# Agent attention with expert rows on one core: the order of the instructions as a literal list instead of a list scheduler with a table of ranks

## The chip, the cores and the metric

The kernel runs on one core of a Trainium2 chip. The metric is the device time of one execution in microseconds (us); lower is better. The core has five instruction queues that matter here: TensorE (PE in the profile, with its weight loads as PEld), VectorE (DVE), ScalarE (ACT), GpSimd (POOL) and SyncE (SP), which issues almost all transfers. Each queue runs its own instructions strictly in the order in which the program holds them and waits at each for the semaphores it needs.

## The reference, cut to what matters

```python
# q, k, v: 4 x 12608 x 128 fp32; agents: 4 x 49 x 128
a2k    = softmax(scale * agents @ k.T)        # 49 x 12608 per batch, over all keys
agentv = a2k @ v                              # 49 x 128
q2a    = softmax(scale * q @ agents.T)        # 12608 x 49, over the 49 agents
x      = q2a @ agentv                         # 12608 x 128
# then, per batch: the 128 rows of x with the largest x . w_gate get
scores = x @ w_gate
top    = argpartition(-scores, 128)[:128]
out    = x                                    # all other rows as they are
out[top] = x[top] + sigmoid(scores[top]) * (relu(x[top] @ w1) @ w2)   # w1 128x1024, w2 1024x128
```

## The kernel before

**Tiles.** A batch's 12608 tokens are 99 columns of 128 tokens, cut into seven chunks (six of 15 columns, chunk 6 of 9). The inputs lie transposed or padded in HBM, so a chunk of k, q or v is one load of 960 KB (967.5 KB for v; 576 and 580.5 KB for chunk 6) into one of six buffers (`inp`, N_IN = 6), a chunk of the result is one store of 960 KB. There are 84 such loads and 28 such stores.

**Work per chunk.** For a k chunk: two halves of scores, each four matmuls of 32 agents by 480 tokens into one of three PSUM banks (tile `S`); DVE turns each half into `sk` and takes its maximum (`mx`). After all seven chunks of a batch the common maximum `mb` is made on PE and DVE (`mT`, `mB`); POOL then subtracts it from each `sk`, ACT takes the exponent. For a v chunk: 15 steps that sum `av` on PE, two instructions each. After the seventh, a chain of small steps (`pw`, `pp`) gives the weights `ws`. For a q chunk: two halves of `S` again, DVE turns them into `sq` and takes a row maximum (`qm`); POOL subtracts, ACT takes the exponent and a rounded copy `f`, POOL subtracts the copy for the low part of `f`; PE transposes `f` (`fT`, 15 instructions), ACT or DVE copies it out as `ft`. From `ft` and `ws` come the gate scores (`pg`, 15 instructions of 3 columns) and the output (`po`, 30 instructions), which ACT, DVE and POOL scale into `og`, and SP stores. Per batch a selection of the 128 best rows follows (`all`, `gt`, `pc`), and at the end the expert rows (`qT`, `sc`, `eT`, `xT`, `xe`, `ph`, `py`), whose results POOL scatters into the output (`out<-ey`) after the batch's stores have landed.

**What sets the order.** All these steps are first recorded as operations with their dependencies (class `Recorder`), 1466 in all. `place` then runs a list scheduler over them: it keeps a price of each operation, a price of a change from one kind of PE work to another (`switch`), a model of TensorE's clock (`Clock`) and of the transfers, and at each moment starts on each free engine the ready operation with the smallest rank. The rank is a number per step and engine from the table `RANKS`, less STICK if the operation is of the kind that the engine did last. The operations are then issued in that order, all from line 1435, so that every row of the profile has that line:

```python
    order = place(rec, urgency, SLACK, STICK)
    ...
    with tc.manual_schedule():
        for op in order:
            for call, args, kwargs in op.calls:
                call(*args, **kwargs)
```

The prices decide the order while the program is built; nothing of them is executed on the chip.

## Time and profile before

| | us |
|---|---|
| three runs of the kernel before | 289.36, 289.97, 291.24 (median 289.97) |
| the profiled execution, its own time | 289.3 |
| its span, from first to last instruction | 287.4 |
| TensorE busy in the span | 266.9 (93%) |
| DVE, ACT, POOL busy | 224.3, 171.6, 183.4 |
| moved over the span | 106.68 MB, 371 GB/s on average |

All later rows are of that one profiled execution; 1.9 us of its time lie outside its span. A row of the profile says how long a group of instructions kept an engine busy; what it had waited for stands in brackets behind it, after an arrow. A row that waits for nothing in brackets began when the instruction before it on that engine let it.

### The profile page before, as it was taken

How to read it: one execution, taken by the hardware profiler on the slowest of the kernel's cores; microseconds unless marked ns; L12 is line 12 of the kernel's file. 1: busy time of each engine (PE TensorE's matmuls, PEld its weight loads, DVE VectorE, ACT ScalarE, POOL GpSimd, SP SyncE). 2: the span in 40 equal slices, each digit the busy share in tenths (PEclk: the TensorE clock that was granted, in tenths of full speed). 3: DMA queues.
4: the chain of work that ended last, by engine and by line, in shares of the span. 5: the costliest groups of instructions: out<-in, count | busy, mean ns of one | idle time of the engine just before them, and what ended most of it. 6: DMA issues, size and time to landing. Idle time of an engine off the chain costs nothing.

```text
span 287.4 us, 8559 instructions
## 1 busy us (share of the span) xinstructions
PE 266.9 (93%) x3524; PEld 176.3 (61%) x3524; DVE 224.3 (78%) x517; ACT 171.6 (60%) x313; POOL 183.4 (64%) x152
## 2 busy tenths in 40 slices
PE   1985798999999999999999999999999999999992
PEld 0221235594557645536455974656798789898992
DVE  1897897977999888997788979558925869998730
ACT  1004156553168965518496988979979854975500
POOL 8014799894189999119998329998422234784723
PEclk9999799999999999999999999889999999999997
DMA  7999999999999999999999999999813585999981
GB/s 281 424 408 419 422 426 415 422 417 422 418 421 391 380 423 410 408 421 412 418 423 419 421 422 414 413 420 373 320 52 148 222 349 220 414 413 408 419 372 48
DMA packets 18203, 106.68 MB, mean 371 GB/s; under 512 B 2032, under 2 KB 3440, under 8 KB 18160
## 3 DMA queue, kind: packets, MB, share of 16 engines
q1 hardware_dynamic: 17760, 105.42, 90.1%
q8 instruction: 30, 0.49, 0.7%
q0 software_dynamic: 256, 0.52, 0.5%
q10 hardware_dynamic: 144, 0.13, 0.1%
q14 instruction: 13, 0.11, 0.1%
HBM read 79.85 MB, written 26.21 MB: 369 GB/s over the span
## 4 chain that ended last, share of the span: by engine, by line
PE 65%; POOL 12%; DMA 9%; ACT 7%; DVE 3%; issue 3%; POOLq 0%; ACTq 0%
PE S L1435 24%; PE av L1435 13%; PE po L1435 13%; PE fT L1435 6%; POOL sk L1435 5%; DMA xT<-kT 4%; DMA out<-og 3%; POOL f L1435 3%; PE pg L1435 2%; PE all L1435 2%; ACT gt L1435 2%; PE ph L1435 2%; POOL sq L1435 2%; DMA ag_sb<-agT 2%; ACT ft L1435 2%
## 5 line engine op out<-in xcount | busy, mean ns | idle before, releaser
L1435 PE MATMUL S<-xT,ag_sb 128*32 128x480 f32 (+1 forms) x896 | 102.4, 572 | 10.8 <-DMA ag_sb<-agT 6.0
L1435 POOL TENSOR_TENSOR sq<-sq,qm 128x735 f32<-128x735 f32 (+1 forms) x42 | 56.9, 1368 | 34.9 <-DVE qm L1435 27.8
L1435 PEld LDWEIGHTS <-ft 128*128 128x128 f16 x1188 | 59.1, 98 | 15.1 <-issue 13.3
L1435 POOL TENSOR_TENSOR f<-sq,f 128x735 f16<-128x735 f32 (+1 forms) x28 | 42.7, 1527 | 23.5 <-ACT f L1435 21.2
L1435 PEld LDWEIGHTS S<-xT,ag_sb 128*32 128x32 f32 x896 | 23.5, 111 | 54.1 <-issue 24.6
L1435 PE MATMUL po<-ws,ft 128*128 128x128 f16 x792 | 53.5, 220 | 0.5 <-ACT og L1435 0.4
L1435 POOL TENSOR_TENSOR sk<-sk,mb 128x735 f32<-128x735 f32 (+1 forms) x28 | 47.2, 1703 | 8.8 <-DVE mb L1435 8.8
L1435 PE MATMUL av<-v,sk 128*64 128x129 f32 x792 | 49.9, 275 | 0.4 <-DMA v<-va 0.4
L1435 PEld LDWEIGHTS av<-v,sk 128*64 128x64 f32 x792 | 44.5, 136 | 8.5 <-DMA v<-va 3.6
L1435 ACT COPY ft<-fT 128x896 f16<-128x896 f16 (+2 forms) x49 | 43.7, 896 | 8.8 <-PE fT L1435 8.6
L1435 DVE STREAM_TRANSPOSE sq<-S 128x480 f32<-128x480 f32 (+1 forms) x56 | 35.5, 639 | 11.6 <-POOL f L1435 8.4
L1435 DVE STREAM_TRANSPOSE sk<-S 128x480 f32<-128x480 f32 (+1 forms) x56 | 35.1, 635 | 6.3 <-PE S L1435 3.5
L1435 DVE TENSOR_REDUCE qm<-sq 128x15 f32<-128x735 f32 (+1 forms) x42 | 36.1, 865 | 1.2 <-ACT sq L1435 0.7
L1435 ACT ACTIVATE sq<-sq,lift 128x735 f32<-128x735 f32 (+1 forms) x28 | 25.0, 891 | 19.5 <-POOL sq L1435 19.3
L1435 DVE TENSOR_REDUCE mx<-S 128x1 f32<-128x480 f32 (+1 forms) x56 | 33.0, 607 | 3.1 <-PE S L1435 2.9
L1435 POOL TENSOR_TENSOR og<-og,r 128x512 f32<-128x512 f32 (+1 forms) x26 | 24.3, 944 | 14.1 <-ACT og L1435 13.9
L1435 PEld LDWEIGHTS <-f 128*128 128x128 f16 x396 | 22.9, 98 | 12.2 <-issue 7.6
L1435 ACT ACTIVATE sk<-sk 128x735 f32<-128x735 f32 (+1 forms) x28 | 22.4, 799 | 12.4 <-POOL sk L1435 12.2
L1435 PE MATMUL fT<-idh,f 128*128 128x128 f16 x396 | 28.8, 220 | 0.8 <-POOL f L1435 0.8
L1435 ACT CAST f<-sq 128x735 f16<-128x735 f32 (+1 forms) x28 | 22.2, 793 | 11.1 <-POOL sq L1435 10.5
L1435 ACT ACTIVATE og<-po,iv 128x512 f32<-128x512 f32 (+1 forms) x28 | 18.0, 663 | 12.6 <-PE po L1435 11.5
L1435 DVE SCALAR_TENSOR_TENSOR gt<-all,top,minus 128x512 bf16<-128x512 f32 x32 | 23.6, 739 | 0.9 <-PE all L1435 0.5
(131 smaller groups left out, 251.2 us busy)
## 6 DMA issues: line engine op xcount, KB each, us to landing
v<-va SPq DMA_DIRECT2D x24, 967.5 KB, 8.8
xT<-kT SPq DMA_DIRECT2D x24, 960.0 KB, 9.1
xT<-qT SPq DMA_DIRECT2D x24, 960.0 KB, 9.0
out<-og SPq DMA_DIRECT2D x24, 960.0 KB, 6.4
v<-va SPq DMA_DIRECT2D x4, 580.5 KB, 6.9
xT<-kT SPq DMA_DIRECT2D x4, 576.0 KB, 8.8
xT<-qT SPq DMA_DIRECT2D x4, 576.0 KB, 9.1
out<-og SPq DMA_DIRECT2D x4, 576.0 KB, 5.6
```

The lines of the kernel that those rows point to most:

```text
L1435: call(*args, **kwargs)
```

## The change

The list scheduler, its clock model and the table of ranks are removed. In their place stands a literal list of 1466 numbers, the recorded operations in the order in which they are issued. `place` now only looks the operations up and asserts that each comes after what it depends on. The recorded operations and their shapes are the same, and so are the prices in `price` (which no longer set anything at build time). One dependency is written out: the copy into `f` now names the two memsets that clear the `f` buffers once.

```diff
-SLACK = 0.0
-STICK = 10922.517314977244
-HALF = ("po", "fT", "pg")
[...]
-def place(rec, urgency, slack=0.0, stick=0.0):
...
-RANKS = {
-    ('setup', 0): {"ACT": -7704.603, "POOL": -40854.573, "DVE": -34695.979},
...
+ORDER = (
+    409, 6, 10, 12, 3, 0, 9, 131, 132, 133, 134, 135, 16, 122, 136, 17, 58, 59, 18, 19, 61, 137, 60, 20, 22,
...
+def place(rec):
+
+    order, done = [rec.ops[i] for i in ORDER], set()
+    for op in order:
+        assert op.deps <= done, op.label
+        done.add(op.seq)
+    assert len(done) == len(rec.ops)
+    return order
...
+    zeros = set()
     for i in range(N_F):
         f = qp.tile([P, TMAX, P], F16, tag="f", name=f"f0_{i}", bufs=N_F)
-        nc.gpsimd.memset(f, 0.0)
+        zeros.add(nc.gpsimd.memset(f, 0.0).seq)
...
-        copy(f[:, :n, :A], d["q", c][:, :n, :A])
+        copy(f[:, :n, :A], d["q", c][:, :n, :A]).deps.update(zeros)
...
-    order = place(rec, urgency, SLACK, STICK)
+    order = place(rec)
```

In the rows of order below, a name is a tile, then its chunk, then its half (for `S`), then a running number that sets the batches apart; `xT` is a load of k or q, `v` one of v, and x4 or x15 stands for that many matmuls in a row.

On PE, where the first v chunks of batch 1 are summed (`av_277`), before:

```order
L1435 MATMUL S_0_0_374<-xT_0_373,ag_sb 32x480 x4
L1435 MATMUL S_0_1_375<-xT_0_373,ag_sb 32x480 x4
L1435 MATMUL av_277<-v_0_276,sk_0_242 64x129 x15
L1435 MATMUL all_0_232<-idf,top_226 128x128 x4
L1435 MATMUL S_1_0_378<-xT_1_377,ag_sb 32x480 x4
L1435 MATMUL av_277<-v_1_278,sk_1_246 64x129 x15
L1435 MATMUL av_277<-v_2_279,sk_2_250 64x129 x15
L1435 MATMUL S_3_0_322<-xT_3_321,ag_sb 32x480 x4
L1435 MATMUL S_3_1_323<-xT_3_321,ag_sb 32x480 x4
L1435 MATMUL S_1_1_379<-xT_1_377,ag_sb 32x480 x4
```

The same place on PE, now:

```order
L1123 MATMUL S_2_1_383<-xT_2_381,ag_sb 32x480 x4
L1123 MATMUL S_3_0_322<-xT_3_321,ag_sb 32x480 x4
L1123 MATMUL av_277<-v_0_276,sk_0_242 64x129 x15
L1123 MATMUL av_277<-v_1_278,sk_1_246 64x129 x15
L1123 MATMUL av_277<-v_2_279,sk_2_250 64x129 x15
L1123 MATMUL av_277<-v_3_280,sk_3_254 64x129 x15
L1123 MATMUL pc_234<-c_0_228,idf 128x8
L1123 MATMUL pc_234<-c_0_229,idf 128x8
L1123 MATMUL S_3_1_323<-xT_3_321,ag_sb 32x480 x4
L1123 MATMUL S_4_0_331<-xT_4_330,ag_sb 32x480 x4
L1123 MATMUL S_0_0_505<-xT_0_504,ag_sb 32x480 x4
```

Four v chunks that stood in three runs, with a fourth chunk further on, now stand in one run of 60 steps; the last row is the first half of k chunk 0 of batch 3, whose load `xT_0_504` stood later before.

On SP, the loads that belong to this stretch, before:

```order
L1435 DMA v_0_276<-va 128x1935
L1435 DMA xT_2_312<-qT 128x1920
L1435 DMA xT_0_373<-kT 128x1920
L1435 DMA v_2_279<-va 128x1935
L1435 DMA v_1_278<-va 128x1935
L1435 DMA xT_3_321<-qT 128x1920
L1435 DMA v_5_282<-va 128x1935
L1435 DMA v_3_280<-va 128x1935
```

On SP, the same stretch now:

```order
L1123 DMA v_3_280<-va 128x1935
L1123 DMA xT_3_321<-qT 128x1920
L1123 DMA v_0_276<-va 128x1935
L1123 DMA v_1_278<-va 128x1935
L1123 DMA v_2_279<-va 128x1935
L1123 DMA xT_4_330<-qT 128x1920
L1123 DMA xT_0_504<-kT 128x1920
```

The four v loads of the run now stand within five loads of each other, one other load between them.

On SP, the last loads and the weights of the experts (`w_held`), before:

```order
L1435 DMA xT_4_591<-qT 128x1920
L1435 DMA w_held<-w 128x896
L1435 DMA xT_6_609<-qT 128x1152
L1435 DMA w_held<-w 128x7x128
L1435 DMA xT_3_582<-qT 128x1920
L1435 DMA v_0_537<-va 128x1935
L1435 DMA out<-og_5_660 128x1920
L1435 DMA v_4_542<-va 128x1935
```

On SP, the end of the loads now:

```order
L1123 DMA xT_5_600<-qT 128x1920
L1123 DMA v_5_543<-va 128x1935
L1123 DMA v_6_544<-va 128x1161
L1123 DMA out<-og_0_669 128x1920
L1123 DMA w_held<-w 128x896
L1123 DMA w_held<-w 128x7x128
L1123 DMA out<-og_4_655 128x1920
L1123 DMA out<-og_6_665 128x1152
```

The two loads of `w_held`, 448 KB each, moved behind the last load of the inputs.

Of the kernel before, what the change touches and what calls it, by code (L numbers as in the profile page):

```python
# [28 lines left out]
A = 49  # L29
# [19 lines left out]
SLACK = 0.0  # L49
STICK = 10922.517314977244  # L50
# [202 lines left out]
HALF = ("po", "fT", "pg")  # L253
WINDOW, STAY, RISE = 3413.333, 0.45, 0.76
WORK = {"S": 1.0, "av": 0.89, "po": 0.93, "pg": 0.25, "fT": 0.8, "all": 0.83, "ph": 0.9}
RATE, GATHER, SCATTER = 408.0, 6500.0, 2400.0


def switch(a, b):

    if a in HALF and b in HALF:
        return 10.0
    return 160.0 if a == "av" else 100.0 if a == "S" or b in ("S", "av") else 50.0


def lag(a, b):

    if a.engine == b.engine:
        return 0.0 if a.engine == "PE" else a.tail
    return a.tail + 70.0  # L270


class Clock:


    def __init__(self):
        self.window, self.did, self.full = 0, 0.0, False

    def cost(self, op, t):
        while t >= (self.window + 1) * WINDOW:  # L280
            self.full = self.did >= (STAY if self.full else RISE) * WINDOW
            self.window, self.did = self.window + 1, 0.0
        few = op.kind == "pg"
        c = op.cost * (1.0 if self.full or few else 2.0)
        over = max(0.0, t + c - (self.window + 1) * WINDOW)
        self.did += (c - over) * WORK.get(op.kind, 0.5)
        if over:
            self.full = self.did >= (STAY if self.full else RISE) * WINDOW
            self.window, self.did = self.window + 1, over * WORK.get(op.kind, 0.5)
        return c  # L290


def place(rec, urgency, slack=0.0, stick=0.0):

    ops = rec.ops
    users, takes = {}, [[] for _ in ops]
    for op in ops:
        for name in sorted(op.uses):
            if name not in users:
                takes[op.seq].append(rec.rings[name][0])  # L300
            users.setdefault(name, []).append(op)
    rank = [(urgency(op.tag, op.engine), op.seq) for op in ops]
    room = {ring: bufs for ring, bufs in rec.rings.values()}
    left = {name: len(u) for name, u in users.items()}
    after = [[] for _ in ops]
    missing = [len(op.deps) for op in ops]
    for op in ops:
        for d in op.deps:
            after[d].append(op)
    ready = [0.0] * len(ops)  # L310
    queue = {e: [op for op in ops if op.engine == e and not op.deps] for e in ENGINES.values()}
    free = dict.fromkeys(queue, 0.0)
    last = dict.fromkeys(queue, "")
    times, ends, order = [0.0], [], []
    line, clock = 0.0, Clock()
    while len(order) < len(ops) or ends:
        if not times:
            raise RuntimeError("no instruction can begin")
        now = heapq.heappop(times)
        while ends and ends[0][0] <= now + 1e-6:  # L320
            op = ops[heapq.heappop(ends)[1]]
            for x in after[op.seq]:
                more = slack if x.engine == "PE" and op.engine != "PE" else 0.0
                ready[x.seq] = max(ready[x.seq], op.end + lag(op, x) + more)
                missing[x.seq] -= 1
                if not missing[x.seq]:
                    queue[x.engine].append(x)
                    heapq.heappush(times, ready[x.seq])
            for name in op.uses:
                left[name] -= 1  # L330
                if not left[name]:
                    room[rec.rings[name][0]] += 1
        for e, waiting in queue.items():
            if free[e] > now + 1e-6:
                continue
            best = None
            for op in waiting:
                if ready[op.seq] > now + 1e-6:
                    continue
                key = rank[op.seq]  # L340
                if op.kind == last[e]:
                    key = (key[0] - stick, key[1])
                if best is not None and key >= best[0]:
                    continue
                need = takes[op.seq]
                if all(room[r] >= need.count(r) for r in need):
                    best = (key, op)
            if best is None:
                continue
            op = best[1]  # L350
            waiting.remove(op)
            order.append(op)
            for r in takes[op.seq]:
                room[r] -= 1
            op.start = max(now, free["POOL"]) if op.two else now
            cost = op.cost
            if e == "PE":
                if last[e] != op.kind:
                    op.start += switch(last[e], op.kind) if last[e] else 50.0
                cost = clock.cost(op, op.start)  # L360
            last[e] = op.kind
            free[e] = op.end = op.start + cost
            if op.kind == "dma_start":
                line = max(line, op.start + 1800.0) + op.size / RATE
                op.end = line + 1700.0
            elif op.size:
                op.end += GATHER if op.label.startswith("xq") else SCATTER
            heapq.heappush(ends, (op.end, op.seq))
            heapq.heappush(times, op.end)
            heapq.heappush(times, free[e])  # L370
    return sorted(order, key=lambda op: (op.start, op.seq))


RANKS = {
    ('setup', 0): {"ACT": -7704.603, "POOL": -40854.573, "DVE": -34695.979},
# [9 lines left out]
    ('kmax', 0): {"DVE": 41091.545, "PE": 58712.794},  # L385
    ('exp', 0, 0): {"POOL": -88028.326, "ACT": 169482.5},
    ('exp', 0, 1): {"POOL": -22401.104, "ACT": 321716.736},
    ('exp', 0, 2): {"POOL": 70975.178, "ACT": 315931.785},
    ('exp', 0, 3): {"POOL": 58294.679, "ACT": 304754.866},
    ('exp', 0, 4): {"POOL": 39134.622, "ACT": 334237.156},  # L390
    ('exp', 0, 5): {"POOL": 51140.999, "ACT": 225861.786},
    ('exp', 0, 6): {"POOL": 55847.904, "ACT": 305110.098},
    ('v', 0, 0): {"SP": 11990.05},
    ('av', 0, 0): {"PE": 42293.51},
    ('v', 0, 1): {"SP": 20852.403},
    ('av', 0, 1): {"PE": -95203.721},
    ('v', 0, 2): {"SP": 25732.307},
    ('av', 0, 2): {"PE": 48113.417},
    ('v', 0, 3): {"SP": 26879.58},
    ('av', 0, 3): {"PE": 36554.066},  # L400
    ('v', 0, 4): {"SP": -154.989},
    ('av', 0, 4): {"PE": -244316.769},
    ('v', 0, 5): {"SP": 27655.575},
    ('av', 0, 5): {"PE": 87914.589},
    ('v', 0, 6): {"SP": 28400.238},
    ('av', 0, 6): {"PE": 38896.804},
    ('fin', 0): {"DVE": -136605.102, "PE": -175038.306, "POOL": 41207.367, "ACT": 135592.531},
    ('q', 0, 0): {"SP": -22705.261, "PE": 83217.232, "DVE": 73912.386},
    ('qe', 0, 0): {"POOL": 74676.234, "ACT": 353340.888, "DVE": 25400.62},
    ('turn', 0, 0): {"PE": 110425.037, "DVE": 86067.107, "ACT": 171382.578},  # L410
    ('gate', 0, 0): {"PE": 26353.217},
    ('q', 0, 1): {"SP": -23034.369, "PE": 53477.308, "DVE": -145606.484},
    ('qe', 0, 1): {"POOL": 82352.64, "ACT": 322967.816, "DVE": 37860.525},
    ('turn', 0, 1): {"PE": 83936.752, "DVE": 87178.494, "ACT": 316575.984},
    ('gate', 0, 1): {"PE": 21674.402},
# [227 lines left out]
    ('expert', 2): {"POOL": 38822.733, "PE": 214325.217, "DVE": -26426.609, "ACT": 335914.832},  # L643
    ('expert', 3): {"POOL": -240553.185, "PE": 107739.067, "DVE": -50621.084, "ACT": 308149.546},
}


def urgency(tag, engine):

# [864 lines left out]
```

## Rows read from the trace of the kernel before

**Rows 1.** The page's parts 1 and 2: busy time, then 40 slices

```profile
PE 266.9 (93%) x3524; PEld 176.3 (61%) x3524; DVE 224.3 (78%) x517; ACT 171.6 (60%) x313; POOL 183.4 (64%) x152
...
PE   1985798999999999999999999999999999999992
...
PEclk9999799999999999999999999889999999999997
DMA  7999999999999999999999999999813585999981
```

**Rows 2.** Waits, matmuls of PE alone, 60 to 250 us: total, times, longest

```profile
PE eT L1435 <- ACT ft L1435: 0.4, 1, 0.4
PE po L1435 <- ACT og L1435: 0.4, 1, 0.4
PE fT L1435 <- POOL f L1435: 0.3, 1, 0.3
PE all L1435 <- DVE top L1435: 0.2, 1, 0.2
```

**Rows 3.** Timeline of PE: start, busy, instructions merged while tile and operation stay

```profile
88.72 3.52 PE L1435 MATMUL av<-v,sk 128*64 128x129 f32 x60
92.18 2.62 PE L1435 MATMUL S<-xT,ag_sb 128*32 128x480 f32 x24
94.73 0.62 PE L1435 MATMUL fT<-idh,f 128*128 128x128 f16 x8
95.28 1.98 PE L1435 MATMUL av<-v,sk 128*64 128x129 f32 x30
97.19 1.01 PE L1435 MATMUL fT<-idh,f 128*128 128x128 f16 x15
98.13 1.01 PE L1435 MATMUL S<-xT,ag_sb 128*32 128x480 f32 x8
99.08 0.56 PE L1435 MATMUL fT<-idh,f 128*128 128x128 f16 x7
...
119.14 1.00 PE L1435 MATMUL fT<-idh,f 128*128 128x128 f16 x15
119.98 1.34 PE L1435 MATMUL pg<-ws,ft 128*128 128x3 f16 x45
```

**Rows 4.** Stretches: length, busy time (count) by engine, PEclk, DMA share, GB/s

```profile
56.00:64.00 8.00, 8.00 (x140) 7.48 (x134) 6.01 (x12) 4.80 (x9) 7.75 (x6) 1.00 1.02 420
180.00:190.00 10.00, 9.70 (x162) 5.68 (x154) 5.99 (x9) 9.06 (x12) 9.84 (x9) 0.83 1.04 417
...
216.00:232.00 16.00, 15.50 (x257) 13.22 (x254) 11.90 (x33) 12.94 (x25) 5.18 (x5) 1.00 0.49 197
244.00:278.00 34.00, 33.96 (x460) 30.87 (x457) 25.89 (x65) 21.38 (x51) 20.55 (x22) 1.00 1.01 415
278.00:282.00 4.00, 3.95 (x33) 3.75 (x32) 1.74 (x8) 0.80 (x2) 2.99 (x3) 1.00 0.47 184
```

**Rows 5.** Waits of SP's queue, and the page's part 6 for k loads

```profile
SPq L1435 <- PE S L1435: 80.3, 43, 7.0
...
SPq L1435 <- PE av L1435: 36.3, 20, 3.5
...
xT<-kT SPq DMA_DIRECT2D x24, 960.0 KB, 9.1
```

**Rows 6.** Stores issued from 240 us on: count, size, median us from issue to landing

```profile
out<-og SPq DMA_DIRECT2D x13, 960.0 KB, 6.5
out<-og SPq DMA_DIRECT2D x3, 576.0 KB, 6.5
```

**Rows 7.** SP's timeline: the first of these stores

```profile
243.28 2.65 SPq L1435 DMA_DIRECT2D out<-og  x2
```

**Rows 8.** The end: timeline of all engines

```profile
281.56 0.39 PE L1435 MATMUL py<-w_end,hT 128*128 128x128 f32 x2
281.99 0.35 DVE L1435 SCALAR_TENSOR_TENSOR ey<-py,g,bases 128x128 f32<-128x128 f32 x1 [2.14 <-PE py L1435]
283.16 0.97 POOL L1435 DMA_INDIRECT out<-ey,idx  x1 [1.28 <-DMA out<-og]
```

**Rows 9.** The end: the chain that ended last, start and length

```profile
273.07 9.32 DMA out<-og
...
283.45 0.67 POOL out L1435
```

**Rows 10.** The start: two rows of the timeline that wait for loads

```profile
8.89 0.47 ACT L1435 CAST x<-cst 128x1 bf16<-128x1 f32 x4 [6.43 <-DMA cst<-consts]
...
26.41 1.82 PE L1435 MATMUL S<-xT,ag_sb 128*32 128x480 f32 x16 [1.84 <-DMA xT<-kT]
```

**Rows 11.** Stretches at a low clock, columns as in rows 4

```profile
182.00:184.00 2.00, 2.00 (x75) 2.00 (x73) 0.00 (x0) 2.00 (x3) 2.00 (x2) 1.00 1.06 433
184.00:186.00 2.00, 1.70 (x26) 1.52 (x23) 1.22 (x2) 2.00 (x4) 2.00 (x2) 0.79 1.02 412
186.00:188.00 2.00, 2.00 (x12) 0.34 (x10) 1.61 (x3) 2.00 (x4) 2.00 (x3) 0.50 1.01 420
188.00:190.00 2.00, 2.00 (x35) 0.89 (x31) 1.60 (x2) 1.52 (x2) 2.00 (x2) 0.86 1.01 424
```

**Rows 12.** The page's part 5, DVE on a half of k scores: count | busy, mean ns | idle before

```profile
L1435 DVE STREAM_TRANSPOSE sk<-S 128x480 f32<-128x480 f32 (+1 forms) x56 | 35.1, 635 | 6.3 <-PE S L1435 3.5
...
L1435 DVE TENSOR_REDUCE mx<-S 128x1 f32<-128x480 f32 (+1 forms) x56 | 33.0, 607 | 3.1 <-PE S L1435 2.9
```

More of the change, by code (lines that the diff above doesn't have):

```diff
@@ L250, in price @@
         op.two = op.two or two
-HALF = ("po", "fT", "pg")
[L254 to L270, printed above, removed]
@@ L273 @@
[L273 to L290, printed above, removed]
@@ L293, in place @@
-def place(rec, urgency, slack=0.0, stick=0.0):
[L295 to L371, printed above, removed]
@@ L648, in urgency @@
-def urgency(tag, engine):
-    return RANKS.get(tag, {}).get(engine, 0.0)
+ORDER = (
[74 rows of a table added]
+)
+def place(rec):
[5 more added lines that the diff above has]
+    return order
 def const_layout(capacity):
```

240 lines of the change are left out of this document (removed), and 103 rows, old and new, of tables (ORDER, RANKS).

## The prediction, made before the changed kernel ran

> **What bounds the kernel now.** I read the page's busy times and its 40 slices first [rows 1]. TensorE is busy for 266.9 of 287.4 us, no other engine above 224.3. In the slices TensorE shows 9 from the eighth to the last but one; it has gaps only in the first seven and in the last. Transfers show 9 (saturated) from the second slice to about the 28th, then fall to 1 and 3, and are at 9 again for six slices towards the end. So I asked next what TensorE waits for between 60 and 250 us: its matmuls waited four times, 1.3 us in all [rows 2]. From there to its last instruction at 281.95 us [rows 8] TensorE works back to back, and what it works through sets the end.
>
> Busy is not the same as useful there, and the timeline of TensorE shows it [rows 3]. Read the starts, not the lengths. One half of scores (8 instructions) before other work takes 98.13 to 99.08, 0.95 us; three halves in a row take 92.18 to 94.73, 2.55 us. So a further half costs 0.80 us and the end of a run of scores 0.15 us, whatever its length. Thirty `av` instructions before other work take 95.28 to 97.19, 1.91 us; sixty take 88.72 to 92.18, 3.46 us. So a further thirty cost 1.55 us and the end of a run 0.36 us. Fifteen transposes `fT` take 0.94 us before scores (97.19 to 98.13) and 0.84 us before `pg` (119.14 to 119.98): fp16 work (`fT`, `pg`, `po`) that is followed by fp32 work pays 0.10 us, and fp16 kinds among each other pay almost nothing. TensorE pays for each change of kind.
>
> The second thing near the limit is the transfers. From 244 to 278 us they run at 415 GB/s, share 1.01 [rows 4], for the stores; the last store takes 9.32 us from its issue at 273.07 to 282.39 [rows 9], and the last scatter waits for it, not for TensorE's last result, which was ready at 282.34 [rows 8]. The two ends are level.
>
> **The change part by part.** *Runs on TensorE.* The change keeps every instruction, so I counted runs in the two orders, from the last `av` step of batch 0 on (before it TensorE waits for loads anyway). Runs of scores fall from 42 to 30, runs of `av` from 16 to 10, runs of fp16 work from 59 to 46; the rows of order at batch 1's `av` show how. By rows 3: 12 x 0.15 = 1.8, 6 x 0.36 = 2.2, 13 x 0.10 = 1.3, together 5.3 us less work on TensorE. The saved time lies where TensorE waits for nothing, so it moves the end of TensorE, unless new waits eat it: bounds 0 and -5.3. I take all of it, since in rows 2 the whole stretch waits 1.3 us.
>
> *The start.* The first load is now q chunk 0 instead of k chunk 0; the six k chunks and two q chunks that follow are as many. What counts is how far SP's loads run ahead of the work. At q chunk 1 of batch 1 SP has moved 29.6 MB in the old order and 28.5 in the new, 2.7 us at 420 GB/s [rows 4]; the work of TensorE ahead of its first use, by the durations of rows 3, is 55.6 and 52.8 us, 2.8 less. So TensorE arrives there with the same delay: 0, between -1.0 and +1.5 (a load's wait as in rows 10, 1.84 us, less or once more). The table `cst` moves from third to tenth on SP, and ACT's fifth instruction waits for it; behind it stand the copy into `f` of q chunk 0 and all of ACT. Before, ACT idled 6.43 us for it [rows 10] at no harm. The ten loads are 8.9 MB, moved by some 24 us at the rate of rows 4; copy and low part take ACT and POOL about 2.5 us more; TensorE reaches these transposes only after the last k chunk, 9.9 MB, some 26 us, two halves of scores and the maximum, so not before 29 us. Covered by 2.5 us: 0. The memsets that POOL now does between two subtractions lie under the same loads: 0.
>
> *The last loads.* `w_held`, 0.92 MB, moves behind the last v chunk, so the inputs end 2.2 us sooner. TensorE has 62 to 64 us of work behind its last v chunk, 67 before. Neither gains by itself, since TensorE's work, not the landing, sets when it gets there: 0, but it makes room for the 5.3 us.
>
> *The drain of the stores.* From 243.28 us [rows 7] sixteen stores leave, 13 of 0.983 MB and 3 of 0.59 [rows 6]: 14.6 MB at 415 GB/s are 35.1 us, to 278.4, and rows 4 show the rate falling right there. That is 3.6 us before TensorE's end, and the last store lands 4.0 us after it. In the new order I summed TensorE's work behind each store by the same durations. Two places are tighter: twenty stores (18.5 MB, 44.6 us) begin with 49.8 us of work behind the first, old 49.8 with one store fewer; five full and one small (5.5 MB, 13.3 us) begin with 17.7 us, old five full with 18.8. With the 1.5 to 3.3 us from the last `po` of a chunk to its store's issue, the full rate ends 1.9 to 3.0 us before TensorE's end instead of 3.6. The drain gives back 0.6 to 1.7; I take 1.2, the middle.
>
> *The clock.* The granted clock is 1.00 nearly everywhere, but 0.50 (1.2 GHz) from 186 to 188 us and between in the slices beside it [rows 11]: (0.21 + 0.50 + 0.14) x 2 = 1.7 us lost, after a stretch of 69 `pg` instructions of three columns and some transposes. Another such fall, in the fifth slice of rows 1, lies in the waits of the start. The new order has a comparable stretch of `pg` at the same place (45, a few `po`, 54): I keep the fall, 0, between -1.7 and +1.7.
>
> Sum against the profiled execution: 289.3 - 5.3 + 1.2 = 285.2. The median of the runs shown lies 0.7 above it, 289.97: 289.97 - 4.1 = 285.9.
>
> **The rivals.** *Nothing is gained* (288.5 to 290). What TensorE saves it spends waiting: its runs are longer, so the three banks of scores, DVE and ACT are hit in bursts. For it: DVE is at 78%, and a k half takes it 0.64 + 0.61 = 1.25 us [rows 12] against 0.80 on TensorE; two new runs are six halves long. Against: a run of three halves in rows 3 shows no stall, and rows 2 show hardly any wait on DVE. The Trainium skill has a rule that leads to the same time: its page "TensorE: Matmul & The Clock Gate", section "Back-to-back issue gap", gives a matmul's spacing from its own columns and weight load, with nothing for the kind ahead of it, so that joining runs would save nothing. Rows 3 speak against it with 0.36 us at each end of an `av` run, and the sum is made by them.
>
> *More is gained* (283 to 284.7). The stores begin sooner than my sum has them, so nothing is given back: 284.7; and without the fall of rows 11, 283.0. For it: between 216 and 232 us the transfers are half idle (0.49) [rows 4]. Against: the last stores are closer together than before.
>
> *The clock falls once more* (287.6). The new order joins `fT` and `po` into longer fp16 runs. Rows 11 show one fall after such a stretch, price 1.7 us. [...] Here the clock stays at 1.00 from 56 to 64 us, with two runs of 15 transposes in it [rows 4], so I give it little.
>
> *Slower, by slots held* (293). SP issues a load when TensorE frees one of six buffers, 63 waits, 117 us [rows 5]; a load takes 9.1 us to land, and at 0.983 MB each 415 GB/s need four in flight. In the new order `v_3`, loaded before `v_0` to `v_2`, is used after them, so four of the six buffers hold v chunks when the run of 60 begins, and the load `xT_0_504` holds another for 21 us of work between its two halves. If only two are in flight, the transfers run dry for about one load, 2.4 us, at each of the three runs of 60: +7.2, so 285.9 + 7.2 = 293.1. It decides from the point where the share of the transfers falls below 0.9 around these runs. Against: in the old order a run of 40 steps between two others lies in 56 to 64 us, at share 1.02 [rows 4], and q chunk 2 of batch 3 held its buffer for 11 us near 180 us, at 1.04.
>
> **How the numbers follow.** Forecast 285.9, its own range 284.5 to 287.8: 0.45. More gained: 0.17. Nothing gained: 0.20. Clock: 0.06. Slots: 0.12. About 1%, 2.9 us, is what a measurement of this kernel can tell from no change. Faster by over that (below 287.1): 0.39 of the forecast's 0.45, and 0.17, 0.56 with a rest of 0.01 of the clock's, 0.57. Slower by over that (above 292.9): 0.07 of the slots' 0.12 and 0.03 of the nothing's, whose waits can be longer than the gain: 0.10. Within: 0.33. The range from 282.8 to 291.0 leaves out the slots rival and the outer ends of the others, about 2 in 10.
>
> **What would show it.** TensorE's busy time should fall by about 5 us and its last instruction come near 276.7; `av` runs of 60 should take 3.46 us; waits of its matmuls from 60 us on should stay under 3 us. The transfers should stay at 1.0 until about 205 us, and the last store should land 1 to 3 us behind TensorE's end. I am wrong if TensorE's waits after 60 us grow by several us, on loads (slots) or on DVE and ACT (bursts), or if the store that lands last comes 4 us or more after TensorE.

## The result, and the profile after

The changed kernel takes **285.83 us** (median of 4 runs, 285.31 to 286.26), the old one on the same chip 289.74 (4 runs, 289.36 to 291.24): ratio 0.985, interval 0.982 to 0.989. The forecast was 285.9, range 282.8 to 291.0. The profiled execution of the changed kernel took 285.31, its span is 283.4 against 287.4.

The page of the changed kernel, parts 1 and 2, answers to [rows 1]:

```profile
PE 258.7 (91%) x3524; PEld 175.7 (62%) x3524; DVE 226.3 (80%) x517; ACT 171.3 (60%) x313; POOL 183.8 (65%) x152
...
PE   1866699999999999999999999999999999999991
...
PEclk9999999999999999999999999999999999999997
DMA  7999999999999999999999999999644999899980
```

TensorE is busy 8.2 us less, and both falls of its clock are gone (in [rows 1] the fifth slice showed 7, slices 26 and 27 showed 8). The span shrinks by 4.0 only, so something was given back. The waits of matmuls, total, times, longest, from 60 to 250 us (answers to [rows 2]), then from 0 to 60 us:

```profile
PE av L1123 <- DMA v<-va: 1.1, 3, 0.5
PE S L1123 <- DMA xT<-kT: 1.1, 2, 0.7
PE fT L1123 <- POOL f L1123: 0.6, 2, 0.3
...
PE S L1123 <- DMA ag_sb<-agT: 6.1, 1, 6.1
PE S L1123 <- DVE mx L1123: 4.0, 4, 2.4
PE mB L1123 <- DVE dg L1123: 1.5, 1, 1.5
```

Where the old order waited 1.3 us, the new one waits 3.4, and 2.2 of it are loads, which the old one did not wait for at all. Up to 60 us TensorE now waits 7.0 us for VectorE (3.2 before) and 0.9 us for loads of k and q (3.2 before, among them the 1.84 of [rows 10]); the 6.1 us for `ag_sb` were there before.

The timeline of TensorE, answers to [rows 3]: the runs of `av` are as long as forecast, and their prices are the same.

```profile
89.78 3.52 PE L1123 MATMUL av<-v,sk 128*64 128x129 f32 x60
93.62 3.52 PE L1123 MATMUL av<-v,sk 128*64 128x129 f32 x60 [0.32 <-DMA v<-va]
97.08 0.61 PE L1123 MATMUL pc<-c,idf 128*128 128x8 f32 x4
...
156.60 6.83 PE L1123 MATMUL av<-v,sk 128*64 128x129 f32 x120
163.36 2.79 PE L1123 MATMUL S<-xT,ag_sb 128*32 128x288 f32 x32
```

From 93.62 to 97.08 sixty instructions take 3.46 us. The joined run at 156.60 takes 6.76 to the next start; four runs of thirty would be 4 x 1.91 = 7.64.

Stretches of the changed kernel, columns as in [rows 4]: the place of the old fall ([rows 11]) and the stores.

```profile
188.00:190.00 2.00, 2.00 (x63) 2.00 (x61) 1.80 (x3) 1.87 (x3) 2.00 (x2) 1.00 0.98 382
190.00:192.00 2.00, 2.00 (x68) 2.00 (x66) 0.75 (x1) 1.71 (x3) 2.00 (x3) 1.00 1.04 431
240.00:274.00 34.00, 33.93 (x433) 30.90 (x432) 26.05 (x67) 19.40 (x48) 23.34 (x26) 1.00 0.97 396
274.00:278.00 4.00, 2.85 (x22) 2.35 (x20) 0.96 (x4) 0.80 (x2) 2.06 (x3) 1.00 0.31 109
```

The end, timeline of all engines, answers to [rows 8]:

```profile
276.85 0.39 PE L1123 MATMUL py<-w_end,hT 128*128 128x128 f32 x2
277.27 0.35 DVE L1123 SCALAR_TENSOR_TENSOR ey<-py,g,bases 128x128 f32<-128x128 f32 x1 [1.52 <-PE py L1123]
277.90 0.97 POOL L1123 DMA_INDIRECT out<-ey,idx  x1 [1.36 <-DVE ey L1123]
```

The last scatter no longer waits for a store (`out<-og` in [rows 8]) but for TensorE's last result. TensorE ends at 277.24, 4.7 us earlier than before; from there to the end of the span are 6.2 us, where they were 5.5.

So the books close as -8.2 (busy) + 3.5 (idle ahead of TensorE's end, 18.5 against 15.1) + 0.7 (behind it) = -4.0.

The falls of the clock that are gone do not make the gain. Of all executions on record, on several chips, thirteen of the old kernel had a mean granted clock of 0.997 or more; they took 288.64 to 291.46 us, 289.58 in the median. The four such executions of the changed kernel took 285.04 to 285.55.

### The profile page after: what moved, and what is told of

Read it like the earlier page. It is cut to its first block, busy times and chain, and to the rows that moved or that the text cites. A ratio compares the mean times of both kernels' runs of the same rounds, so it can differ in the third digit from the quotient of the medians.

```text
span 283.4 us, 8570 instructions
## 1 busy us (share of the span) xinstructions
PE 258.7 (91%) x3524; PEld 175.7 (62%) x3524; DVE 226.3 (80%) x517; ACT 171.3 (60%) x313; POOL 183.8 (65%) x152
## 4 chain that ended last, share of the span: by engine, by line
PE 64%; DMA 17%; DVE 9%; issue 3%; POOL 3%; ACT 1%; POOLq 0%; DVEq 0%
PE S L1123 23%; PE po L1123 13%; PE av L1123 10%; DMA v<-va 9%; DMA xT<-kT 6%; PE fT L1123 5%; PE pg L1123 3%; PE all L1123 3%; PE py L1123 3%; PE ph L1123 2%; DVE gt L1123 2%; DMA ag_sb<-agT 2%; DVE sk L1123 2%; DVE sq L1123 2%; DVE qm L1123 1%
## 5 line engine op out<-in xcount | busy, mean ns | idle before, releaser
L1123 PE MATMUL S<-xT,ag_sb 128*32 128x480 f32 (+1 forms) x896 | 97.8, 557 | 14.1 <-DMA ag_sb<-agT 6.1
L1123 PEld LDWEIGHTS <-ft 128*128 128x128 f16 x1188 | 57.9, 97 | 9.3 <-issue 8.4
L1123 PEld LDWEIGHTS S<-xT,ag_sb 128*32 128x32 f32 x896 | 24.4, 110 | 60.3 <-issue 25.8
L1123 PE MATMUL po<-ws,ft 128*128 128x128 f16 x792 | 52.4, 219 | 0.5 <-ACT x L1123 0.4
L1123 ACT COPY ft<-fT 128x896 f16<-128x896 f16 (+2 forms) x49 | 42.9, 894 | 13.9 <-PE fT L1123 13.9
L1123 PE MATMUL av<-v,sk 128*64 128x129 f32 x792 | 47.8, 274 | 1.1 <-DMA v<-va 1.1
L1123 DVE STREAM_TRANSPOSE sq<-S 128x480 f32<-128x480 f32 (+1 forms) x56 | 34.5, 633 | 11.7 <-PE S L1123 11.5
L1123 ACT ACTIVATE gt<-all,top 128x512 bf16<-128x512 f32 x32 | 22.0, 687 | 3.1 <-PE all L1123 2.6
```

## The experiments

A few of them set out from the changed order, a few from the old one. All keep the recorded operations unless the diff says otherwise. "Changed" is the changed kernel; in `av`, one step of the program is two instructions of the profile.

**Joined runs taken apart.** Ten edits on TensorE alone, two of them:

```diff
  av_277<-v_1_278 x15
+ S_3_1_323 x4
  av_277<-v_2_279 x15
  av_277<-v_3_280 x15
- S_3_1_323 x4
...
- av_277<-v_4_281 x15
+ av_277<-v_4_281 x10
  S_5_0_340 x4
+ av_277<-v_4_281 x5
```

> The changed order with ten of its joined runs on TensorE taken apart again (from 90 us on): seven more runs of scores, eight more of av, three more of fp16 work; nothing else moves. Theory 'kinds' (a run's end costs 0.15, 0.36 and 0.10 us, and most of the gain came from fewer ends): 4.2 us more work on TensorE, the end 3.2 to 4.2 us later than the changed kernel's 285.8, since at most 1 us of it can hide under the waits for loads before 145 us; 289.0 to 290.0. Rival 'clock' (the gain is the two falls of the granted clock that are gone, and the ends of runs cost nothing): 0, between 285 and 286.5.

It took 295.53 us (294.32 to 296.41), ratio to the old kernel 1.016 (1.010 to 1.021). The changed kernel did not run on this chip; by the ratios (1.016 against 0.985) it is nine above changed, more than either theory has it. Its waits from 60 to 250 us begin so:

```profile
PE S L1123 <- DVE sk L1123: 3.0, 1, 3.0
PE po L1123 <- ACT gt L1123: 2.0, 1, 2.0
PE po L1123 <- DVE og L1123: 1.9, 2, 1.7
PE av L1123 <- DMA v<-va: 1.6, 1, 1.6
```

Pieces moved forward had to wait for their bank or input. So most of the nine is new waits, and the time decides nothing about ends; TensorE's busy time does. It is 262.0 us against 258.7, and 2.9 of these 3.3 us lie behind 40 us, where the cuts are (235.78 against 232.87 from the same matmul on). That is less than 4.2, and the timeline shows why. Thirty `av` instructions cut into 10 and 20 took 0.78 (133.14 to 133.92) and 1.25 us (134.86 to 136.11), 2.03 where one run takes 1.91: a short run is cheap, and such a cut costs 0.12 here and up to 0.15 in the other places of this kind, not 0.36.

**The same without waits.** Twelve edits, with pieces that are ready early or wanted late, such as:

```diff
- po_3_4_652 x8
  S_6_0_479 x4
  S_6_1_480 x4
+ po_3_4_652 x8
```

> The changed order with twelve joined runs taken apart, now by pieces whose inputs are ready long before or whose results are wanted late, so that no new wait should come of it: eight more runs of scores, seven more of av, seven more of fp16 work. At 0.15, 0.36 and 0.10 us that is 4.4 us; three of the av cuts are 10 and 20 instructions instead of 30, and such a cut took 0.13 us instead of 0.36 in the run before, so 3.7 us. Theory 'kinds': TensorE busy 258.7 + 3.7 = 262.4, the time 3 to 4 us above the changed kernel on this chip. Rival 'clock' (ends of runs cost nothing): busy as before at 258.7, the time within 0.7 us of the changed kernel.

289.09 us (287.61 to 290.93, 10 runs), ratio to the old 0.996 (0.992 to 1.000); changed, on the same chip, 285.72. That is 3.4 us above it, as 'kinds' has it. The work says so too. From the same matmul on to TensorE's end, here and in the changed kernel on the same chip, both at a clock of 1.00:

```profile
41.43:282.26 240.83, 235.98 (x3302) 167.99 (x3298) 195.89 (x460) 164.28 (x303) 162.45 (x131) 1.00 0.94 375
```

```profile
40.52:277.41 236.89, 232.80 (x3302) 168.37 (x3298) 195.92 (x460) 163.72 (x303) 162.20 (x131) 1.00 0.95 382
```

TensorE is busy 3.2 us longer, for the forecast 3.7. That the time fits as well is in part luck: in the two profiled executions it is 3.2 of work, 0.8 of added waits and 0.9 from the start, where the clock fell in this one, less 1.1 because the stretch behind TensorE's end is shorter in this build (5.1 against 6.2 us, see below), together the 3.7 by which the spans differ.

The rival falls. The Trainium skill's page "TensorE: Matmul & The Clock Gate", section "Back-to-back issue gap", which has nothing for the kind ahead, would have forecast 0 here; the measurement decides against it.

**The changed kernel again.**

> The changed kernel itself, unaltered, beside the three others on one chip, so that they can be compared with it: 0.985 of the old one.

285.72 us (285.04 to 286.80), ratio 0.985 (0.980 to 0.990).

**pg in a row.** The chunks 0, 2 and 4 of batch 2's `pg` move behind the transposes and the output that parted them:

```diff
- pg_431 (chunks 0, 2, 4) x45
  fT x15, po_4_4 x8
+ pg_431 (chunks 0, 2, 4) x45
  pg_431 (chunks 5, 1, 6, 3) x54
```

> The changed order with batch 2's pg steps (45 and 54 instructions with transposes and output between them, at 188 to 192 us) put in one row of 99. The count of runs stays. Theory 'few columns let the clock fall': a fall to 0.50 as in the old kernel appears within some us behind the row and the end comes 1.7 us later, 287.5. Rival 'the fall has another cause': the clock stays at 1.00 and the time at 285.8, within 0.5.

288.00 us (287.25 to 289.80, 8 runs), ratio to the old kernel 0.989 (0.985 to 0.994). The changed kernel did not run on this chip: it is 2.2 us above changed as measured elsewhere, 1.2 to 1.4 by the ratios. Every execution had a mean granted clock of 0.988 or less, the changed kernel's ten had 0.986 to 0.999. Stretches around the row, which stands at 192.5 to 195.2 us:

```profile
192.00:194.00 2.00, 1.92 (x64) 1.92 (x64) 0.83 (x2) 2.00 (x4) 2.00 (x2) 1.00 1.01 423
194.00:196.00 2.00, 2.00 (x57) 1.91 (x54) 0.62 (x2) 0.57 (x2) 2.00 (x3) 0.76 1.03 429
196.00:198.00 2.00, 2.00 (x18) 0.80 (x20) 1.76 (x6) 2.00 (x3) 1.84 (x2) 0.50 1.01 418
198.00:200.00 2.00, 2.00 (x27) 1.04 (x20) 1.67 (x3) 1.03 (x2) 0.57 (x1) 0.89 0.82 251
```

The clock goes to 0.50 (1.2 GHz) right behind the row, and by these lines the fall costs (0.24 + 0.50 + 0.11) x 2 = 1.7 us, as forecast. Two new waits ahead of the row (0.50 and 0.21) add 0.7; as the row did not come without them, this run does not part the two causes.

**The old order with its pg row parted, twice.** In the first try 30 of the 69 moved back and a half of scores came between two transposes; in the second a half of scores that stood ahead of the row parted it:

```diff
- S_1_1_566 x4
  fT x7, po_2_0 x8
  pg_431 x24
+ S_1_1_566 x4
  pg_431 x45
```

> The old order with its row of 69 pg instructions at 182 us broken up: 39 stay, 30 move behind four more pieces of work, and one half of scores moves between the two transposes; the count of runs is the same. Theory 'few columns let the clock fall': the fall at 184 to 190 us is gone and the time is 1.7 us below the old kernel, ratio 0.994. Rival 'the fall comes from the wait there (0.30 us) or is chance': the fall stays, the ratio is 1.00.

> The old order with its row of 69 pg instructions at 182 us parted, this time by one half of scores that stood ahead of it (24 pg, four scores instructions twice the length of a pg row, 45 pg); one run more of scores and one of fp16 work, 0.25 us. The earlier try made a new wait of 1.8 us in the same place, which is idle time too. Theory 'little work on TensorE lets the clock fall, be it pg or idle': with neither, no fall behind it, the time 1.4 us below the old kernel, ratio 0.995. Rival 'the fall belongs to this place whatever stands there': it stays, ratio 1.001.

The first took 291.48 us (289.50 to 293.64), ratio 1.004 (0.999 to 1.008): the scores waited 1.82 us for their bank, TensorE stood idle in that place instead of doing `pg`, and the clock lay at 0.50 from 187 to 194 us. The second took 289.94 (288.46 to 292.53), ratio 1.000 (0.996 to 1.004), and in its profile the fall is gone:

```profile
184.00:186.00 2.00, 1.92 (x55) 1.75 (x52) 0.54 (x1) 1.86 (x3) 2.00 (x2) 1.00 1.00 410
186.00:188.00 2.00, 2.00 (x37) 1.09 (x38) 1.97 (x4) 2.00 (x4) 2.00 (x3) 1.00 1.01 411
188.00:190.00 2.00, 1.96 (x18) 0.32 (x19) 1.83 (x3) 1.90 (x4) 2.00 (x2) 1.00 1.02 428
```

So the fall does not belong to the place. In these profiles it came with rows of 69 and 99 `pg` that had waits of 0.30 and 0.71 us beside them, and with a wait of 1.82 us; it did not come where both row and wait were gone, nor in the changed kernel with 45 and 54 `pg` and no wait. A long row without any wait was not tried, so which of the two it takes stays open. From the first of the two halves of scores to the next `av` the same work takes 10.66 us instead of 11.77, with 0.25 of new ends in it, so the fall and the wait of 0.30 were worth 1.35 us there. But the measured time did not follow: 1.4 was forecast, and against 289.37 for the old kernel on the same chip nothing can be seen. This profiled execution of the old order has no fall at all, and its span is still 287.2.

It is the better yardstick for the books, since a TensorE that is busy at half clock covers what would be waits. Its busy times, then the first 60 us here, in [rows 1]'s execution (with a fall) and in the changed kernel:

```profile
PE 264.1 (92%) x3524; PEld 176.0 (61%) x3524; DVE 224.0 (78%) x517; ACT 171.9 (60%) x313; POOL 183.3 (64%) x152
...
0.00:60.00 60.00, 44.38 (x465) 18.98 (x467) 48.15 (x92) 19.93 (x31) 38.81 (x38) 1.00 0.98 402
```

```profile
0.00:60.00 60.00, 46.55 (x467) 19.22 (x469) 48.16 (x93) 20.05 (x31) 38.94 (x38) 0.97 0.99 403
```

```profile
0.00:60.00 60.00, 45.48 (x479) 18.52 (x480) 47.81 (x87) 19.73 (x28) 39.42 (x34) 1.00 0.99 404
```

TensorE is idle for 15.6 us there without a fall and for 13.5 with one. Against this yardstick the changed kernel is busy 5.4 us less (5.3 forecast for the ends, and 0.25 for the two that this build has more: 5.5), idle 1.1 less in the first 60 us (14.5 against 15.6), idle 2.0 more from there to TensorE's end, and 0.7 longer behind it: -5.4 - 1.1 + 2.0 + 0.7 = -3.8, which is 283.4 - 287.2.

**The start.** The old order on all engines up to batch 0's `pw`, then the new one; and the same with `tri_i` made early:

```diff
  CAST tri_b<-cst
+ TENSOR_TENSOR tri_i<-cst,idf
...
- TENSOR_TENSOR tri_i<-cst,idf
```

> The old order of everything that the changed order does up to batch 0's pw (68 us), on all engines, then the changed order unaltered. Runs of TensorE cost 0.3 us more. Theory 'the new start loses 1.1 us in waits': 285.8 - 1.1 + 0.3 = 285.0 if the clock stays up in the start; 286.1 or a little more if the fall at 30 to 36 us comes back with the old start and TensorE has no wait behind it that takes it up. Rival 'the start is free, the loads set when TensorE gets on': 285.8 either way, and the waits for loads between 60 and 150 us grow by what the start saves.

> The old order up to batch 0's pw, then the changed one, as in the earlier run, with one thing more: the small table tri_i is made by DVE at 9 us, as in the old order, instead of at 100 us, where it took 1.85 us and TensorE's pc waited 1.3 us for it. Theory 'the new start loses 1.1 us': that wait goes, and the time is 1.0 to 1.5 us below the changed kernel on this chip. Rival 'the start is free, the loads set when TensorE gets on': within 0.5 us of the changed kernel, with 1 us more of waits for loads before 150 us.

285.61 us (284.96 to 286.22) and 284.73 (283.94 to 286.89); ratios 0.981 (0.976 to 0.986) and 0.982 (0.976 to 0.987). The first lies between its forecasts and decides nothing by itself. In it `pc` waited 1.3 us for `tri_i`:

```profile
L1123 DVE TENSOR_TENSOR tri_i<-cst,idf x1: 1851/1851/1851, 100.8 to 100.8; 128x128 bf16<-128x128 f32 x1
```

The 284.73 look like the 1.0 of the theory, but the trace says otherwise: TensorE ends at 278.11, *later* than in the changed kernel on the same chip (277.41); what is shorter is the stretch behind it, 5.1 against 6.2 us. So these two executions show no loss by the new start. I had compared with an old profile whose fall at 30 to 36 us hid its waits.

**w_held ahead of the last inputs.**

```diff
+ DMA w_held<-w 128x896
+ DMA w_held<-w 128x7x128
  DMA xT_3_582<-qT 128x1920
...
- DMA w_held<-w 128x896
- DMA w_held<-w 128x7x128
```

> The changed order with the two loads of w_held (0.92 MB) put back ahead of the last nine loads of the inputs. By the prediction (TensorE's work, not the landing, sets when it gets to the last chunks): 285.8, no new waits. Rival 'the end of the inputs counts': the inputs end 2.2 us later, TensorE waits for the last v or q chunks, up to 288.0.

286.14 us (284.96 to 287.65), ratio 0.982 (0.976 to 0.987). Waits for loads from 60 us on are 3.0 us against 2.2, but the last of them ends at 147 us, long before the moved loads leave (182.75 us): no sign of the rival's 2.2 us.

**The drain.**

```diff
+ m = n // 2 if b in (2, 3) else n
- nc.sync.dma_start(outs[b][:, j0:j0 + n], o3[:, :n])
+ nc.sync.dma_start(outs[b][:, j0:j0 + m], o3[:, :m])
```

> The changed kernel with the last fourteen stores (batches 2 and 3) writing only the first half of their columns: half of these rows of the result are left out, so it measures the drain alone. The prediction's term 'the drain gives back 1.2 us': with half the bytes the end comes 1.2 us earlier, 284.6. Theory from the trace after (the last scatter waits for TensorE's last result, not for a store): 285.7, TensorE's end within 0.3 us of the changed kernel's 277.2 to 277.4.

With half the columns of the last fourteen stores left out it took 285.79 us (285.24 to 287.84), ratio 0.985 (0.979 to 0.992): no gain. The transfers of the last stretch are busy for 0.58 of their time instead of 0.97, and the kernel ends no sooner:

```profile
240.00:274.00 34.00, 34.00 (x452) 31.16 (x452) 27.06 (x69) 20.64 (x50) 23.05 (x25) 1.00 0.58 226
```

In its profiled execution (287.84, with a fall of the clock in the start) TensorE ended at 279.81, so 277.2 is not seen there; that the drain takes nothing is read from the times.

**Behind TensorE's end.** One memset changes its engine:

```diff
- nc.vector.memset(eps, 1e-9)
+ nc.gpsimd.memset(eps, 1e-9)
```

> The changed kernel with one of its setup memsets (eps, 128x1) given to GpSimd instead of VectorE; the order is the same. In the traces so far the time from TensorE's last instruction to the end is 6.2 to 6.4 us in the four builds with 581 recorded instructions on VectorE (14 packets in the instruction queue q14) and 5.0 to 5.5 us in the six with 579 or 580 (13 packets). Theory 'code': with 580 the end comes 1.1 us earlier at the same end of TensorE, 284.6. Rival 'chance': 6.2 us as before, 285.7.

285.23 us (283.69 to 286.85), ratio 0.983 (0.978 to 0.988). TensorE's end to the span's end is 5.1 us here (279.86 to 285.0). The packets are 14 as before, so they are not the sign. The edit takes one instruction from VectorE and gives one to GpSimd. Over all 14 profiles this stretch is 6.2 to 6.5 us in the five with 581 recorded instructions on VectorE and 5.1 to 5.5 in the nine with 579 or 580; GpSimd's count parts them less well (231 in one of the nine as in the five). The row of the last branch (L1129) in the changed kernel and here: duration, then first and last start of GpSimd's four semaphore steps there.

```profile
L1129 POOLq EVENT_SEMAPHORE  x4: 17/42/43, 278.4 to 281.4; - x4
```

```profile
L1129 POOLq EVENT_SEMAPHORE  x4: 17/42/43, 281.0 to 282.9; - x4
```

3.0 us against 1.9. That the code's place in memory does it is my reading, not shown.

The times of the six executions part by the clock: 283.69, 283.97 and 284.57 at 0.995 and more, 285.89 to 286.85 at 0.993 and less. The profiled one is of the latter, with falls between 28 and 39 us behind waits of 2.54 and 1.13 us. So the last one filled the waits:

```diff
+ warm = psX.tile([P, 512], F32, tag="X", name="warm")
+ for n in (7, 5):
+     with rec.group():
+         for _ in range(n):
+             nc.tensor.matmul(warm[:, :P], ones_f, ones_f, start=True, stop=True)
```

> The changed order with eps on GpSimd as in the run before, and twelve fp32 multiplications of ones by ones (128 columns each, result unused) put into two waits of TensorE in the start: seven ahead of the scores that wait 2.4 us near 25 us, five ahead of mB that waits 1.5 us near 32 us; 3.1 us of idle work by the 0.26 us that such a multiplication takes in py. In the executions of all kernels so far the granted clock of a whole run lies between 0.976 and 1.0, and those of the same kernel at 0.995 and more are 1 to 2.5 us shorter; in the profiles the difference is falls to 0.5 between 30 and 50 us, behind these waits. Theory 'idle TensorE lets the clock fall': the falls go, every execution lies at 0.993 or more, median 284.2 (the three of the run before at 0.995 and more took 283.7 to 284.6). Rival 'the falls come anyway': 285.2 as the run before, or 0.3 more where the filling delays the scores.

284.71 us (284.30 to 287.67), ratio 0.983 (0.979 to 0.987). Five of six executions lie at 0.996 to 1.000 and take 284.30 to 285.48; one lies at 0.992 with 287.67. Five of the changed kernel's ten executions lay at 0.996 or more as well, so six executions don't show that the filling makes falls rarer, and one fell all the same. Each of the last two beats the old kernel clearly; that they beat the changed one, by 0.5 and 1.0 us in the median and on other chips, is not shown.

## Why the prediction was right

The forecast of 285.9 met 285.83. Its main step is what the runs show; that the sum came within 0.1 us is luck. It had +1.2 for the drain, which measured 0. It did not have the waits (+2.0), the start (-1.1) and the stretch behind TensorE's end (+0.7), which together are +1.6.

- **Runs on TensorE: right, in mechanism and nearly in size.** 5.4 us measured between profiles without falls, for 5.3 forecast and 0.25 more in that build; taking apart what was priced at 3.7 us gave back 3.2 of work. The price is not one per end: a cut of 30 `av` into 10 and 20 costs 0.12 to 0.15. The change joins mostly whole chunks, so this hardly touched the sum.
- **"I take all of it, since the whole stretch waits 1.3 us": wrong by 2.0.** Waits on TensorE from 60 us on grew by 2.0 to 2.4 us (3.4 instead of the "under 3" I had set), most of it for loads between 93 and 144 us. The transfers are at 1.01 of their time from 90 to 144 us and again from 144 to 198 (0.86 at the least in two microseconds); the full rate ends there and not at 205 as forecast. I had counted whether loads keep their distance for one chunk of batch 1 only. That TensorE, faster, runs into the rate of the transfers is likely but was not tried by itself.
- **The start: 0.1 beyond its bounds.** 0 forecast, between -1.0 and +1.5; in the first 60 us TensorE is idle 1.1 less than in an old execution without a fall. `cst` lands at 24.4 us, ACT waits 7.1 us for it, and no transpose waits behind: that cover held.
- **The last loads: 0, as forecast**, as far as the run with `w_held` moved back shows it.
- **The drain: wrong.** 1.2 forecast, 0 measured. The full rate ends at about 274.1 (share 1.01 in the half microsecond before 274.0, 0.66 and 0.39 in the two quarters behind it), 3.1 us ahead of TensorE's end, near the forecast 1.9 to 3.0. What failed is the next step: the last store needed 4 us from there in the old order, and I carried that over. The last store leaves at 270.55 instead of 273.07 and lands in about 6.0 us instead of 9.3, 2.4 us behind the full rate's end and 0.7 us *ahead* of TensorE's, where I had expected 1 to 3 behind it.
- **The clock: "I keep the fall" was wrong.** With 45 and 54 `pg` parted by 23 fp16 instructions there is no fall in the profile, with 99 in a row there is one, and the mean clock was 0.988 or less in all eight executions. The sum did not need this step: with its fall gone the old order was no faster. The error was inside the 1.7 allowed.
- **Not foreseen:** 0.7 us behind TensorE's end.

Of the rivals, 'nothing is gained' needed waits on VectorE and ScalarE, and from 60 to 250 us there are none on VectorE and 0.6 us on ScalarE. 'Slots' is not what came: around the long runs at 90 and 157 us the transfers keep a share of 1.01 (0.93 at the least in two microseconds); at the third, from 198 us, they do fall below the 0.9 of its test, to 0.56 and 0.21 for four microseconds, but the inputs are nearly through there and no wait for a load follows. 'The clock falls once more' did not come in the profiled executions.

## What to carry to other kernels

Where TensorE works without a wait, count the ends of runs of a kind in two orders and price them from starts in the timeline; joining whole chunks took 5 us of work off TensorE here, of which new waits, most of them for loads, took back 2. Don't read waits off a profile with a clock fall in it: here TensorE's idle time in the first 60 us was 13.5 us with a fall and 15.6 without; take an execution without one as the yardstick. Compare TensorE's work from the same matmul on, since the stretch behind its end can differ by a microsecond between builds. And a piece of work moved forward in a full order met, in the first run above, a bank or buffer that was not yet free: move such things as are ready early, or nothing.

## What was unexpected of the hardware

- The price of a run's end depends on the run's length: thirty `av` instructions take 1.91 us and sixty 3.46, but ten take 0.78 and twenty 1.25.
- The mean granted clock of one program differs from execution to execution, and the time with it: in the build with `eps` moved, 283.7 to 284.6 us at 0.995 and more, 285.9 to 286.9 below. The one of these that was profiled (0.987) had its falls in the start.
- The stretch behind TensorE's end was 5.1 us with one memset moved from VectorE to GpSimd, 6.2 before, with no work of the kernel in the difference. The cause is open.
- A 128x128 sum of two fp32 operands on VectorE took 0.29 us at 100.3 us in the changed kernel and 1.85 us at 100.8 in the one with the old start, where one of GpSimd's lasted from 99.65 on with a second behind it, to 102.53. In the changed kernel GpSimd was no less busy (98.86 to 101.91 with two instructions), but `tri_i` started just where the first of them ended; what holds the operation up was not tried by itself.
